# Moving the stores of converted weight tiles from SyncE's to GpSimd's DMA queue in an attention and two-layer-MLP kernel

## The chip, the cores and the metric

The kernel runs on one core of one Trainium2 chip. A core has five engines that run at the same time, each with its own instruction queue that is worked off strictly in order: TensorE (PE in the profile; its weight loads are PEld), VectorE (DVE), ScalarE (ACT), GpSimd (POOL) and SyncE (SP), which in this kernel does nothing but start transfers. Sixteen DMA engines carry the transfers. What is measured is the time of one execution on the device in microseconds (us); lower is better.

## What is computed

The reference, cut to its core: attention with rotated q and k over 2 batches of 8 heads, 576 tokens of 64 values, then two gated layers on the 1152 tokens of 512 values.

```python
scores = (q_rot @ k_rot.T) / sqrt(D); attn = softmax(scores); x = attn @ v        # 2 x 8 heads
x = x.transpose(0, 2, 1, 3).reshape(1152, 512)
x = ((x @ w_a) * (x @ w_b)) @ w_out                                               # d_ff 1536
h = x @ w_in;  out = (h * tanh(log1p(exp(h)))) @ w_out2                           # d_ff 2048
```

All weights arrive as 64-bit floats, seen by the kernel as pairs of 32-bit words. The host does no arithmetic.

## The kernel before

**Stages.** Tokens are worked batch by batch. From the start to about 100 us the attention of batch 0 runs, with its score tiles transposed by TensorE. From about 100 to 250 us the attention of batch 1 is interleaved with the first gated layer of batch 0 (`layer1(0, ...)`, then `layer2(0, ...)`): here the score tiles are split into two 16-bit halves `pp` by VectorE and transposed by transfers (`pt<-pp`, 36 of them). Then comes the first gated layer of batch 1, and from about 365 us on the last two layers (`hidden_two` and `accumulate`), which end with the output.

**Weights.** `weights` (from line 578) is called for each of 68 tiles of 128x512 values. SyncE loads the 64-bit tile `wr`; VectorE turns it into 32-bit floats `xw` by three instructions (one TENSOR_SCALAR, two SCALAR_TENSOR_TENSOR); a copy of `xw` is stored to a DRAM scratch tile, `ka` for the 24 tiles of layer one, `kb` for the 12 of its second matmul, `kc` for the 32 of the last two layers. These stores (256 KB each) are lines 601 and 607. When the second batch needs the tile, it is loaded from there (`wc<-ka` and so on) and isn't converted again. For the first use the tile is split into a rounded part and a rest: ScalarE writes the one (`w<-xw`), VectorE or GpSimd the other (`w<-xw,w`, the `any_` instruction of `weights`). Until about 250 us `wr` and `xw` have three buffers each: the fourth conversion waits until the first one's store has landed and its split is done.

**The order of the work.** Nothing is issued directly. Every call is recorded by `Plan.record`, with a cost from `Plan.cost`; `Plan.order` then runs a list scheduler over the recorded instructions, with a priority for each, and the instructions are issued to the engines in the order it gives. Instructions recorded on `any_` go to VectorE or GpSimd, by which of the two ends them earlier by the planner's account. Two instructions that read two SBUF tiles are held apart on these two engines (`op.lock`). So a change of where one instruction stands, or of what it costs in the planner, moves others on all engines.

Two names of the rows below: `qkr` are loaded q and k tiles, which are rotated into `qk` by VectorE and GpSimd (`any_` again), and `m` is the row maximum that VectorE takes of each score tile `s`.

Of the kernel before, what the change touches and what calls it, by code (L numbers as in the profile page):

```python
# [41 lines left out]
YM = 1500  # L42
D1 = 6
D4 = 2
LOOK = dict(pe=50, act=0, dve=0, pool=0, sp=0)


# [128 lines left out]
class Plan:  # L176
# [30 lines left out]
    def record(self, engine, method, args, kw):  # L207
        key = engine.key
        out = kw["out"] if "out" in kw else args[0]
        also = kw.pop("also", ())  # L210
        views = [v for v in list(args) + list(kw.values()) if isinstance(v, View)]
        deps, roots = [], []
        for v in views + list(also):
            t = v.root
            assert not t.dead, t.kw
            if t.first is not None:
                deps.append((t.first, False))
            elif t not in roots:
                roots.append(t)
                deps.append((t.pool.opened, True))  # L220
                if t.before is not None and t.before not in roots:
                    deps.append((t.before.first, False))
                if t.frees is not None:
                    t.frees.dead = True
                    deps += [(op, True) for op, *_ in t.frees.seen]
        marks = []
        for v in views:
            write, box = v is out or v is kw.get("accum_out"), v.box()
            for op, b, w, e, a in v.root.seen:
                bank = v.root.pool.space == PSUM and (key == "pe") != (e == "pe")  # L230
                if (write or w or bank) and box[0] < b[1] and b[0] < box[1] and box[2] < b[3] and b[2] < box[3]:
                    if v.root.pool.space == PSUM or v.meets(a):
                        deps.append((op, True))
            marks.append((v, box, write))
        if key == "flex":

            scale = kw["scale"]
            forms = (
                ("act", "activation", args + (AF.Copy,), dict(scale=scale)),
                ("dve", "tensor_scalar_mul", args + (scale,), {}),  # L240
            )
            method, args, kw = forms[0][1:]
        cost, dma = self.cost({"any": "dve", "flex": "act"}.get(key, key), method, out, args, kw, views)
        op = self.new(key, (engine.real, method, args, kw), deps, cost, dma, roots)
        op.wide = key == "pe" and views[1].root.dtype != F16

        ins = [v for v in views if v is not out and v is not kw.get("accum_out")]
        sb = sum(v.root.pool.space != PSUM for v in ins)
        op.lock = key in ("dve", "pool", "any") and (sb > 1 or sb == len(ins) == 1)
        if key == "any":  # L250
            op.costs = dict(dve=cost, pool=self.cost("pool", method, out, args, kw, views)[0])
        elif key == "flex":
            op.costs = {e: self.cost(e, m, out, args, {}, views)[0] for e, m, *_ in forms}
            op.call = {e: (self.real[e], m, a, k) for e, m, a, k in forms}
        for t in roots:
            t.first = op
        for v, b, w in marks:
            t = v.root
            if w and (v.a.flags.contiguous or v.n * v.a.itemsize == b[3] - b[2] or t.pool.space == PSUM):
                t.seen = [  # L260
                    s for s in t.seen if not (b[0] <= s[1][0] and s[1][1] <= b[1] and b[2] <= s[1][2] and s[1][3] <= b[3])
                ]
            t.seen.append((op, b, w, key, v.a))
        return op

    def cost(self, key, method, out, args, kw, views):

        if key == "sp":
            v = views[0]
            if method == "dma_start_transpose":  # L270
                return 1356, 1700
            return 475, int(np.prod(v.a.shape)) * v.a.itemsize / 320
        psum = any(v.root.pool.space == PSUM for v in views if v is not out)
        n = max(v.n for v in views)
        pointers = sum(v.n == 1 for v in views if v is not out) if out.n > 1 or method == "tensor_scalar" else 0
        if key == "pe":
            rhs = kw["rhs"] if method == "matmul" else args[1]
            n = rhs.n
            n *= 1 if rhs.dtype != F32 else 4 if method == "matmul" else 2
            if rhs.a.shape[0] == 64 and rhs.dtype == F32:  # L280
                n /= 2
            return n, n * rhs.a.shape[0] / 128
        if key == "act":
            return n / 1.2 + (51 if psum else 93) + 93 * min(pointers, 1), 0
        if key == "dve":
            fast = method.startswith("tensor_scalar") or method == "tensor_copy"
            if psum:
                return n / 0.96 + 65 + 58 * min(pointers, 1), 0
            return n / (1.92 if fast else 0.96) + 69 + 58 * min(pointers, 1), 0
        if key == "pool":  # L290
            return (n * 2.132 + 132 if method != "memset" else n), 0

    def order(self):
# [17 lines left out]
        while True:  # L311
# [44 lines left out]
            free[e] = start + op.cost  # L356
            if op.lock:
                held[e] = free[e]
            if e == "sp":
                tr = op.call[1] == "dma_start_transpose"  # L360
                d0 = max(dma_free, start + (1300 if tr else 1100))
                dma_free = d0 + op.dma
                if tr:
                    free[e] = max(free[e], dma_free - 1700)
                op.end = dma_free
            else:
                op.end = free[e]
            same, other = self.LAT.get(e, (0, 0))
            if e == "sp":
                same = other = 1000  # L370
            stale |= {"act", "dve", "pool"} if e in ("act", "dve", "pool") else {e}
            for nxt, data in op.after:
# [54 lines left out]
S0_AT = 20  # L427
W3S = 28
HBB = 2
EARLY = 6  # L430
S_AT = 10
GB = 6
# [48 lines left out]
def lo32(ap):  # L481
    return ap.bitcast(F32)
# [3 lines left out]
def kernel(ctx: ExitStack, tc: tile.TileContext, qk, v5, w1, w2, w34, tab, out):  # L486
# [9 lines left out]
        plan.engine(k, e)  # L496
        for k, e in dict(pe=nc.tensor, act=nc.scalar, dve=nc.vector, pool=nc.gpsimd, sp=nc.sync, any=None, flex=None).items()
    )

    def open_pool(name, bufs=1, side="left", space=None):  # L500
        kw = dict(name=name, bufs=bufs)
# [27 lines left out]
    kept = {}  # L529
# [39 lines left out]
    def weights(  # L569
# [5 lines left out]
        if cached is not None and cached in kept:  # L575
            tag = "rawc" if "rawc" in rings else "xw"
            r = rings[tag][0].tile([128, 512], F32, tag=tag, name=f"wc{i}", bufs=rings[tag][1])
            plan.release = 1000 * hold
            sp.dma_start(r, kept[cached])
            plan.release = 0  # L580
        else:
            r = rings["raw"][0].tile([128, 512], I64, tag="raw", name=f"wr{i}", bufs=rings["raw"][1])
            plan.release = 1000 * hold
            sp.dma_start(r, src)
            plan.release = 0
            words = r.bitcast(U32).rearrange("p (n t) -> p n t", t=2)
            lo, hi = words[:, :, 0], words[:, :, 1]
            x = rings["xw"][0].tile([128, 512], U32, tag="xw", name=f"xw{i}", bufs=rings["xw"][1])
            dve.tensor_scalar(x, hi, 3, 0x3FFFFFF8, op0=ALU.logical_shift_left, op1=ALU.bitwise_and)
            dve.scalar_tensor_tensor(x, hi, 0xC0000000, x, op0=ALU.bitwise_and, op1=ALU.bitwise_or)  # L590
            if plain:

                w = w_p.tile([128, 2, 512], F32R, tag="w", name=f"w{i}", bufs=6)
                dve.scalar_tensor_tensor(
                    w[:, 0, :].bitcast(U32), lo, 29, x, op0=ALU.logical_shift_right, op1=ALU.bitwise_or
                )
                if stat is not None:
                    magnitude(lo32(w[:, 0, :]), stat)
                if keep is not None:
                    kept[keep] = d_p.tile([128, 512], F32, tag=f"k{keep}", name=f"k{keep}")  # L600
                    sp.dma_start(kept[keep], lo32(w[:, 0, :]))
                return w
            dve.scalar_tensor_tensor(x, lo, 29, x, op0=ALU.logical_shift_right, op1=ALU.bitwise_or)
            r = x.bitcast(F32)
            if keep is not None:
                kept[keep] = d_p.tile([128, 512], F32, tag=f"k{keep}", name=f"k{keep}")
                sp.dma_start(kept[keep], r)
            if stat is not None:
                magnitude(r, stat)
            if top is not None:  # L610
                dve.tensor_reduce(top, r, axis=AX.X, op=ALU.max, apply_absolute_value=True)
# [958 lines left out]
```

## Time and profile before

| what | value |
|---|---|
| time, median of 3 runs | 561.01 us (559.72 to 561.78) |
| the profiled execution | 559.72 us, of which its span 557.9 us |
| PE busy | 543.5 us (97%) |
| DVE busy | 473.7 us (85%) |
| ACT busy | 356.2 us (64%) |
| POOL busy | 137.0 us (25%) |
| DMA, share of 16 engines | 69.6% on the one queue that the kernel uses |

The profile is of one execution; times count from the first instruction. An engine's busy time counts its arithmetic, not waiting and not the issue of transfers. Matmuls overlap one another, so a busy PE is not PE at its peak rate. Rows of the queue that SyncE works off are marked SPq. A line number says little here: all instructions are issued on one line (398), so the names of the tiles tell them apart; out<-in is what an instruction writes and reads.

### The profile page before, as it was taken

The page shows a single profiled execution, that of the slowest core. Times are in us where ns is not written, and L with a number is a line of the kernel's source. Part 1 is how long each engine was busy: PE and PEld are TensorE (multiplying, and loading weights), DVE is VectorE, ACT ScalarE, POOL GpSimd, SP SyncE. Part 2 cuts the span into 40 slices and gives each one's busy share as a digit, 9 for nine tenths or more (in the row PEclk, how much of TensorE's full clock was granted, in tenths as well). Part 3 has the DMA queues.
Part 4 walks back from the last instruction along what each step waited for, and adds up shares of the span by engine and source line. Part 5 has one row for each costly group of instructions (what it writes and reads, how often), then busy time and mean ns, then how long its engine had stood idle before and what let it go on. Part 6 is the DMA issues. An engine that isn't in the chain of part 4 may idle for free.

```text
span 557.9 us, 11793 instructions
## 1 busy us (share of the span) xinstructions
PE 543.5 (97%) x4416; PEld 429.0 (77%) x4416; DVE 473.7 (85%) x897; ACT 356.2 (64%) x731; POOL 137.0 (25%) x176
## 2 busy tenths in 40 slices
PE   7999999999999999999999999999999999999997
PEld 5777788889898989899777779997666776555553
DVE  5998999999999999976998999879999997554542
ACT  3879788677678786554676764459675545443440
POOL 1677657521221010110003103645420200000000
PEclk8899999999999999999999999999999999999999
DMA  8336456899999999999988379774789555421002
GB/s 317 110 102 214 166 165 177 228 229 218 290 204 241 252 260 241 236 268 376 387 274 278 102 254 344 269 242 147 264 278 326 179 189 200 137 96 60 1 0 94
DMA packets 92200, 117.40 MB, mean 210 GB/s; under 512 B 52080, under 2 KB 58224, under 8 KB 92144
## 3 DMA queue, kind: packets, MB, share of 16 engines
q1 hardware_dynamic: 92144, 116.66, 69.6%
q8 instruction: 34, 0.56, 0.4%
q14 instruction: 22, 0.18, 0.1%
HBM read 77.82 MB, written 27.53 MB: 189 GB/s over the span
## 4 chain that ended last, share of the span: by engine, by line
PE 84%; DVE 8%; ACT 3%; issue 2%; DMA 1%; POOL 1%; SPq 0%; DVEq 0%; ACTq 0%; POOLq 0%
PE l L398 38%; PE acc L398 16%; PE h L398 13%; PE s L398 8%; PE o L398 6%; PE tm L398 2%; DVE m L398 2%; DVE xw L398 1%; PE xt L398 1%; DMA qkr_k<-in_qk_dram 1%; DVE ptm L398 1%; DVE pp L398 1%; DVE wv L398 1%; DVE hb L398 1%; ACT wv L398 1%
## 5 line engine op out<-in xcount | busy, mean ns | idle before, releaser
L398 PE MATMUL l<-x,w 128*128 128x320 f32 (+3 forms) x1152 | 157.8, 294 | 0.0
L398 PE MATMUL acc<-w,g 128*128 128x512 f16 (+1 forms) x432 | 103.4, 384 | 0.0
L398 DVE SCALAR_TENSOR_TENSOR xw<-wr,xw 128x512 uint32<-128x512 uint32 x136 | 95.6, 708 | 1.0
L398 PEld LDWEIGHTS <-wv 128*128 128x128 f16 x672 | 64.7, 98 | 27.9 <-issue 5.9
L398 PE MATMUL l<-ab,w 128*128 128x320 f32 (+1 forms) x576 | 81.3, 299 | 0.1
L398 PEld LDWEIGHTS l<-x,w 128*128 128x128 f32 x576 | 78.2, 190 | 3.0 <-issue 2.7
L398 PEld LDWEIGHTS l<-ab,w 128*128 128x128 f32 x576 | 77.5, 190 | 1.2 <-issue 0.8
L398 PEld LDWEIGHTS <-w 128*128 128x128 f16 x576 | 56.1, 98 | 14.3 <-issue 0.2
L398 PEld LDWEIGHTS <-g 128*128 128x128 f16 x372 | 36.3, 98 | 36.7
L398 DVE TENSOR_TENSOR hb<-h,hb 128x256 f32<-128x256 f32 (+1 forms) x112 | 48.0, 453 | 13.5 <-PE h L398 11.9
L398 PE MATMUL h<-sp,wv 128*128 128x256 f16 (+1 forms) x384 | 57.7, 286 | 0.6 <-DVE hb L398 0.6
L398 DVE TENSOR_REDUCE m<-s 128x1 f32<-128x576 f32 x72 | 51.9, 749 | 4.4 <-PE s L398 3.9
L398 PE MATMUL s<-qk 64*128 64x288 f32 x256 | 44.8, 439 | 2.4 <-DVE qk L398 1.6
L398 ACT ACTIVATE hb<-hb,two_dn 128x512 f32<-128x512 f32 (+1 forms) x32 | 24.8, 775 | 34.1 <-DVE hb L398 34.1
L398 ACT ACTIVATE junk<-xw 128x512 f32<-128x512 f32 x51 | 32.6, 639 | 17.4 <-DVE xw L398 15.4
L398 PE MATMUL h<-y,wv 128*128 128x256 f16 (+1 forms) x288 | 43.3, 286 | 0.3 <-DVE hb L398 0.3
L398 PEld LDWEIGHTS s<-qk 64*128 64x128 f32 x256 | 25.5, 190 | 11.4 <-issue 4.9
L398 ACT ACTIVATE s<-s,m 128x576 f32<-128x576 f32 x36 | 25.3, 716 | 11.5 <-DVE m L398 11.0
L398 DVE TENSOR_SCALAR xw<-wr 128x512 uint32<-128x512 uint32 x68 | 31.7, 477 | 0.5 <-DMA wr<-in_w_dram 0.5
L398 DVE SCALAR_TENSOR_TENSOR g<-hb,g_up,g 128x640 f16<-128x640 f32 (+1 forms) x27 | 24.2, 895 | 6.3 <-ACT g L398 5.8
L398 DVE SCALAR_TENSOR_TENSOR w<-wc,o_up,w 128x512 f16<-128x512 f32 x16 | 11.9, 750 | 20.2 <-ACT w L398 20.1
L398 POOL TENSOR_TENSOR w<-xw,w 128x512 fp32r<-128x512 f32 x10 | 13.6, 1362 | 62.2 <-ACT w L398 59.1
(186 smaller groups left out, 937.5 us busy)
## 6 DMA issues: line engine op xcount, KB each, us to landing
wr<-in_w_dram SPq DMA_DIRECT2D x68, 512.0 KB, 5.3
kc<-xw SPq DMA_DIRECT2D x32, 256.0 KB, 4.2
qkr<-in_qk_dram SPq DMA_DIRECT2D x14, 576.0 KB, 4.5
wc<-kc SPq DMA_DIRECT2D x27, 256.0 KB, 3.7
ka<-xw SPq DMA_DIRECT2D x24, 256.0 KB, 3.1
wc<-ka SPq DMA_DIRECT2D x24, 256.0 KB, 5.3
wt<-kc SPq DMA_DIRECT2D x16, 256.0 KB, 3.9
kwt<-wv SPq DMA_DIRECT2D x8, 512.0 KB, 3.8
```

The source lines that it names most:

```text
L398: getattr(engine, method)(*map(real, args), **{k: real(v) for k, v in kw.items()})
```

## The change

The planner learns that a transfer may be issued from an engine other than SyncE (a table of costs, `ISSUE`), and the two stores in `weights` go to the engine that `STQ` names, which is GpSimd. All 68 stores of converted tiles move; the loads, the transposing transfers, the other stores (the 16 of `kwb` and `kwt`, and the output) stay on SyncE.

```diff
+ISSUE = dict(sp=475, act=350, pool=1000)
...
-        op.lock = key in ("dve", "pool", "any") and (sb > 1 or sb == len(ins) == 1)
+        op.lock = key in ("dve", "pool", "any") and not method.startswith("dma_start") and (sb > 1 or sb == len(ins) == 1)
...
-        if key == "sp":
+        if method.startswith("dma_start"):
...
-            return 475, int(np.prod(v.a.shape)) * v.a.itemsize / 320
+            return ISSUE[key], int(np.prod(v.a.shape)) * v.a.itemsize / 320
...
-            if e == "sp":
+            moves = op.eng != "event" and op.call[1].startswith("dma_start")
+            if moves:
...
-            if e == "sp":
+            if moves:
                 same = other = 1000
...
+STQ = "pool"
...
+    st = dict(act=act, pool=pool, sp=sp)[STQ]
...
-                    sp.dma_start(kept[keep], lo32(w[:, 0, :]))
+                    st.dma_start(kept[keep], lo32(w[:, 0, :]))
...
-                sp.dma_start(kept[keep], r)
+                st.dma_start(kept[keep], r)
```

Since the planner sees a different cost on two engines, the order changes on all of them from the first store on, and some `any_` instructions change sides. SyncE's queue a little after 100 us, before (`pt` are the transposing transfers, `wr` the loads of weights):

```order
L398 DMA_TRANSPOSE pt_1726<-pp_1686 128x9x128
L398 DMA_TRANSPOSE pt_1751<-pp_1701 128x9x128
L398 DMA ka_1775<-xw_1679 128x512
L398 DMA wr_1781<-in_w_dram 128x512
L398 DMA ka_1791<-xw_1690 128x512
L398 DMA wr_1808<-in_w_dram 128x512
L398 DMA vh_1831<-vhl_108 64x8x66 x2
```

and the same place of SyncE's queue now:

```order
L400 DMA_TRANSPOSE pt_1700<-pp_1670 128x9x128
L400 DMA_TRANSPOSE pt_1739<-pp_1696 128x9x128
L400 DMA wr_1760<-in_w_dram 128x512
L400 DMA wr_1823<-in_w_dram 128x512
L400 DMA_TRANSPOSE pt_1838<-pp_1809 128x9x128
L400 DMA_TRANSPOSE pt_1878<-pp_1817 128x9x128
L400 DMA vh_1907<-vhl_108 64x8x66 x2
```

The stores are gone from between the loads, and two transposes now stand ahead of the small copies `vh`. GpSimd's queue between about 190 and 250 us, where layer one of batch 0 ends, before:

```order
L398 TENSOR_TENSOR ab_7_0_2868<-a_sb,ab_7_0_2868 128x256
L398 TENSOR_TENSOR w_2884<-xw_2765,w_2884 128x512
L398 TENSOR_TENSOR ab_8_0_3023<-a_sb,ab_8_0_3023 128x256
L398 TENSOR_TENSOR w_3323<-xw_3250,w_3323 128x512
L398 TENSOR_TENSOR w_3403<-xw_3311,w_3403 128x512
L398 TENSOR_TENSOR w_3714<-xw_3630,w_3714 128x512
L398 TENSOR_TENSOR w_3803<-xw_3746,w_3803 128x512
```

and now, from the same tile of layer one on:

```order
L400 TENSOR_TENSOR ab_8_0_3018<-a_sb,ab_8_0_3018 128x256
L400 DMA ka_3089<-xw_3008 128x512
L400 TENSOR_TENSOR w_3116<-xw_3008,w_3116 128x512
L400 DMA ka_3157<-xw_3061 128x512
L400 DMA ka_3214<-xw_3154 128x512
L400 DMA ka_3315<-xw_3262 128x512
L400 TENSOR_TENSOR w_3334<-xw_3262,w_3334 128x512
L400 DMA kb_3359<-xw_3268 128x512
L400 DMA kb_3458<-xw_3389 128x512
L400 DMA kb_3548<-xw_3484 128x512
L400 DMA kb_3603<-xw_3490 128x512
```

Stores now fill GpSimd's queue there, and of the rests `w<-xw,w` fewer stand on it. Over the whole program the instructions that change sides between GpSimd and VectorE are these, all of them between the first store (60 us) and 250 us: of `w<-xw,w` GpSimd has 8 in place of 10; of `qk<-qkr` 128x576, 4 in place of 6; of `ab<-a_sb,ab` 128x256, 3 in place of 4; of `qkr<-qkr,cs` 128x576, 6 in place of 7; of `qkr<-qkr,cq` 128x576, 8 in place of 6. VectorE has the difference each time.

## Rows read from the trace of the kernel before

**Rows 1.** The page's first part: busy time, share of the span, instructions of each engine
```profile
span 557.9 us, 11793 instructions
PE 543.5 (97%) x4416; PEld 429.0 (77%) x4416; DVE 473.7 (85%) x897; ACT 356.2 (64%) x731; POOL 137.0 (25%) x176
```

**Rows 2.** Stretches: length, busy time of the engines named, clock, DMA share, GB/s
```profile
core 0: us, PE busy (x) PEld busy (x) DVE busy (x) ACT busy (x) POOL busy (x), PEclk, DMA share, GB/s
60.00:250.00 190.00, 186.46 (x1827) 165.91 (x1826) 180.96 (x337) 140.35 (x325) 55.34 (x61) 1.00 0.91 227
60.00:100.00 40.00, 37.84 (x427) 31.70 (x426) 37.81 (x75) 33.02 (x74) 27.63 (x37) 1.00 0.54 171
100.00:160.00 60.00, 58.75 (x534) 52.35 (x535) 58.44 (x102) 43.91 (x104) 14.05 (x13) 1.00 0.98 237
...
260.00:360.00 100.00, 100.00 (x797) 85.09 (x796) 94.51 (x186) 63.14 (x145) 18.11 (x20) 1.00 0.81 283
```

**Rows 3.** Waits of PE and DVE, 60 to 250 us: total, times, longest
```profile
PE s L398 <- DVE pp L398: 1.3, 3, 0.5
PE xt L398 <- POOL xbd L398: 0.9, 1, 0.9
...
DVE a_sb L398 <- PE l L398: 1.6, 4, 0.7
...
DVE xw L398 <- DMA wr<-in_w_dram: 0.5, 1, 0.5
...
DVE qkr L398 <- DMA qkr<-in_qk_dram: 0.4, 1, 0.4
```

**Rows 4.** Longest wait of SyncE's queue, 60 to 250 us: total, times, longest
```profile
SPq L398 <- DVE xw L398: 33.6, 19, 4.5
```

**Rows 5.** Groups of VectorE (x71, x26, x35: 60 to 250 us) and GpSimd: busy, mean ns, idle before
```profile
L398 DVE SCALAR_TENSOR_TENSOR xw<-wr,xw 128x512 uint32<-128x512 uint32 x71 | 50.3, 708 | 0.4
...
L398 DVE TENSOR_TENSOR w<-xw,w 128x512 fp32r<-128x512 f32 x26 | 20.5, 790 | 0.5 <-ACT w L398 0.4
L398 DVE TENSOR_SCALAR xw<-wr 128x512 uint32<-128x512 uint32 x35 | 16.9, 489 | 0.5 <-DMA wr<-in_w_dram 0.5
...
L398 DVE TENSOR_TENSOR qkr<-qkr,cq 128x576 f32<-128x576 f32 x8 | 6.5, 821 | 0.0
L398 DVE TENSOR_TENSOR qkr<-qkr,cs 128x576 f32<-128x576 f32 x7 | 5.3, 767 | 0.4 <-DMA qkr<-in_qk_dram 0.4
L398 DVE TENSOR_TENSOR ab<-a_sb,ab 128x256 fp32r<-128x256 f32 x8 | 4.4, 556 | 0.0
L398 DVE TENSOR_TENSOR qk<-qkr 128x576 f32<-128x576 f32 x1 | 0.8, 752 | 0.0
...
L398 POOL TENSOR_TENSOR w<-xw,w 128x512 fp32r<-128x512 f32 x10 | 13.6, 1362 | 62.2 <-ACT w L398 59.1 <-DVE a_sb L398 3.1
```

**Rows 6.** Tile xw, whole span: duration ns min/median/max, first and last start
```profile
L398 DVE SCALAR_TENSOR_TENSOR xw<-wr,xw x136: 668/684/1262, 57.0 to 457.8; 128x512 uint32<-128x512 uint32 x136
L398 DVE TENSOR_SCALAR xw<-wr x68: 367/421/1656, 56.5 to 456.6; 128x512 uint32<-128x512 uint32 x68
...
L398 DVE TENSOR_TENSOR w<-xw,w x26: 667/687/1796, 80.3 to 248.5; 128x512 fp32r<-128x512 f32 x26
L398 SPq DMA_DIRECT2D ka<-xw x24: 326/339/1343, 60.5 to 200.5; - x24
```

**Rows 7.** Timelines of DVE, SPq and POOL, 104 to 123 us: start, duration, instruction
```profile
111.71 1.66 DVE L398 TENSOR_SCALAR xw<-wr 128x512 uint32<-128x512 uint32 x1
...
122.06 0.41 DVE L398 TENSOR_SCALAR xw<-wr 128x512 uint32<-128x512 uint32 x1
...
116.03 0.57 SPq L398 DMA_DIRECT2D ka<-xw  x1
...
111.12 1.97 POOL L398 TENSOR_TENSOR qkr<-qkr,cs 128x576 f32<-128x576 f32 x1
```

**Rows 8.** The page's DMA issues: count, KB each, median us from issue to landing
```profile
ka<-xw SPq DMA_DIRECT2D x24, 256.0 KB, 3.1
```

## The prediction

> **What bounds the kernel now.** I read the page's first part, then the busy times by stretch, then who waits for whom. PE is busy 97% of the span [rows 1], so at most some 14 us of the 557.9 are PE idle, and part of that is the start. The stores of the change begin at 60 us [rows 6], so I looked from there on. From 60 to 250 us PE is busy 186.5 of 190 us and DVE 181.0 [rows 2]: two engines are nearly full together, with 3.5 and 9.0 us of holes. From 260 to 360 us PE is at 100 of 100 us and DVE at 94.5, so there PE alone sets the pace and passes a delay on unchanged. The waits between 60 and 250 us say the same [rows 3]: PE's longest in total is 1.3 us, for DVE, and none of its waits is for a transfer. DVE waits for transfers twice, 0.5 us for a load of weights and 0.4 us for one of q and k. What DVE has to do between 60 and 250 us is therefore what another instruction there is charged to.
>
> SyncE's queue looks bad at first sight: it stands 33.6 us waiting for a conversion `xw` to end before it can issue a store, with loads and transposes behind it [rows 4]. But a wait counts only if somebody waits for what stands behind it, and rows 3 say that nobody does, but for 0.9 us.
>
> **The change part by part.**
>
> *SyncE's queue loses 68 stores.* 36 of them (24 `ka`, 12 `kb`) lie before 250 us, at 0.34 us of issue each [rows 6], 12.2 us together, plus the 33.6 us of waiting. The loads behind them start earlier, as far as their buffers allow. The gain is bounded by what DVE waits for transfers, 0.9 us, since PE waits for none. I take 0, with −0.9 as the end.
>
> *VectorE gets arithmetic that stood on GpSimd.* By the counts of the order and the means of rows 5: two `w<-xw,w` at 0.790, two `qk` at 0.752, one `ab` at 0.556, one `qkr,cs` at 0.767, and two `qkr,cq` fewer at 0.821. That is 1.58 + 1.50 + 0.56 + 0.77 − 1.64 = +2.8 us of DVE, all between 60 and 250 us. GpSimd loses four instructions net, 4 × 1.36 = 5.4 us by the mean of its `w`.
>
> The two engines also disturb each other. At 111.71 us DVE's TENSOR_SCALAR took 1.66 us in place of its median of 0.42 and ended just after POOL's instruction of 111.12 us, which took 1.97 [rows 6, 7]. Priced by mean against median [rows 5, 6], DVE loses 26 × 0.103 = 2.7 us on `w`, 35 × 0.068 = 2.4 us on TENSOR_SCALAR and 71 × 0.024 = 1.7 us on the other conversions, 6.8 us while POOL is busy for 55.3 us [rows 2]: 0.12 us for each us of POOL. The four instructions that leave POOL so give DVE 5.4 × 0.12 = 0.6 us back.
>
> *GpSimd gets 36 stores before 250 us and 32 after.* No row shows a transfer issued by POOL, so I bound it. From below: a store has no operand that POOL's arithmetic reads, and may cost DVE nothing, 0. From above: it occupies POOL like an arithmetic instruction on a tile of that size, 1.36 us [rows 5], and disturbs DVE at the same rate: 36 × 1.36 × 0.12 = 5.9 us. The nearest row is the same transfer issued by SyncE, 0.34 us [rows 6]: 36 × 0.34 × 0.12 = 1.5 us, which I take. The 32 `kc` stores fall where PE is full and DVE has some 5% to spare [rows 2]; I cost them at 0. If that cover is gone, they are 32 × 0.34 × 0.12 = 1.3 us.
>
> *Buffers.* The `xw` ring holds three tiles, so a store that lands late stops a conversion, and everything behind it on DVE. The store issued at 116.03 us empties the buffer that DVE writes again at 122.06 us [rows 7]. A store lands 3.1 us after its issue [rows 8], so 2.9 us are left, in what is among the tightest of the 36 cases. POOL may delay a store that long without anyone noticing. I cost it at 0.
>
> Here a rule speaks against the change. The trace shows how work of POOL and an instruction of DVE shut each other out for over a microsecond [rows 7]. The Trainium skill, page "SBUF — State Buffer", section "SBUF: two separate sides", says that the descriptors of a DMA issued from GpSimd are written by GpSimd's own cores, which are locked out while VectorE runs an instruction in a two-port mode; under "A bandwidth-pool intuition that's wrong" it tells of such a DMA that took 620 ns alone and 3100 beside one. By it, as an estimate, a store would land 2.5 us later, still inside the 2.9 us left, and the sum would stay as it is. No run shows it yet; it bears on the first rival.
>
> *The sum.* DVE gets +2.8 − 0.6 + 1.5 = +3.7 us between 60 and 250 us. How much reaches the end? At least nothing, if its 9.0 us of holes take it all; at most all. DVE is busy 95% there, nearer to full than to free, and some of the holes are waits for PE (1.6 us in the longest row of rows 3), which shrink as DVE falls behind. I take two thirds, +2.5 us. On the profiled run of 559.72 us (span 557.9 and 1.8 around it) this gives 562.2. That run lies 1.3 us under the median of the three, and a median is what is asked, so the forecast is 561.0 + 2.5 = **563.5 us**. Its own range is 561.3 to 566: at the low end a third of 2.2 (no store term) and half of the 0.9 us of loads saved, at the high end the whole 3.7 with the 1.3 of the `kc` stores.
>
> **The rivals.**
>
> *GpSimd and VectorE get in each other's way, slower.* Every store occupies POOL like a full instruction. Then the store term is 5.9 in place of 1.5, and DVE's plus is 8.1 us, about as much as all its holes, so that most work waits for it and it passes nearly whole: 561.0 + 8.1 = 569.1 us. Such a store decides from about 0.7 us on POOL, where its term of 3.0 brings DVE's plus to 5. It grows if POOL's queue gets late by more than the 2.9 us of the ring, since DVE then stands in front of a conversion: six stores late by half a microsecond beyond that are 3 us more. For it: the 1.66 us of rows 7, and a queue in which stores that wait for DVE now stand ahead of `xbd` and `xn`, which lead to PE's transposes. Against it: POOL is busy only 55 of 190 us [rows 2], and what PE waits for it is 0.9 us, once [rows 3].
>
> *The loosened queue pays, faster.* Loads run ahead, two tiles are converted in a row, and the order that the planner finds for DVE, ACT and PE with less in SyncE's way is the tighter one. What there is to gain is PE's idle time from 60 to 250 us, 3.5 us, of which 2.2 lie before 100 us and 1.3 before 160 [rows 2]. All of it gives 557.5 us. For it: 33.6 us of waiting vanish from SyncE's queue [rows 4]. Against it: DVE has more to do than before, and nobody waits for a load [rows 3]. The Trainium skill, page "Perfetto Trace Analysis", section "DMA Optimizations", holds that it may make sense to give loads to one issuing engine and stores to another; no row here shows it to be worth more than this.
>
> *Nothing moves.* DVE's holes take up what is added, 561.0 us.
>
> **How the numbers follow.** The forecast, 45%; stores that cost POOL and DVE dearly, 25%; faster, 20%; nothing moves, 10%. A measurement of this kernel can tell about 0.5% from no change, so the limits are 558.2 and 563.8. Faster: the second rival, 0.20. Same: the 10% of the last and 28 of the forecast's 45, together 0.38. Slower: the other 17 and the 25 of the first rival, 0.42. To hold the time eight times in ten the range must reach into both rivals: from 556.5 (all of PE's idle time, the 0.9 us of loads and a little) to 572 (the first rival with its ring term).
>
> **What would show it.** Right: DVE's busy time up by 3 to 4 us before 260 us, medians of `w` and TENSOR_SCALAR unchanged, no wait of DVE for a `ka` store, a span longer by 2 to 4 us, all of it there when the first batch's layer one ends. The first rival: means of the conversions well over 0.49 and 0.71 us, or waits of DVE or ACT for POOL or for `ka<-xw`. The second: PE's 3.5 us of idle time gone. I would be wrong altogether with a loss that arises after 260 us, where I cost everything at nothing, or with stores that land far later than 6 us after their issue.

## The result, and the profile after

The changed kernel takes **563.74 us** in the median (563.41 to 566.73), the kernel before 561.1 beside it: ratio 1.0057 with a 95% interval of 1.0032 to 1.0082. A second comparison gave 1.0041 [1.0021, 1.0061]. The change costs 2.3 to 3.2 us. The forecast was 563.5. The number is right; of the steps that led to it, several are not.

The first part of the page after (busy time, share of the span, instructions), to be held against [rows 1]:

```profile
span 561.8 us, 11874 instructions
...
PE 545.5 (97%) x4416; PEld 429.9 (77%) x4416; DVE 473.7 (84%) x901; ACT 355.7 (63%) x731; POOL 170.1 (30%) x240
```

DVE has its four additional instructions (901 for 897), and yet its busy time is the same to a tenth. It should have risen by 3.7 us. POOL has 33.1 us more: the profile counts the issue of a store as busy time on GpSimd, which it does not on SyncE. The 68 stores are 38.2 us of it (18.0 and 13.7 in the rows below, and 6.5 for the 12 `kb`); POOL's arithmetic fell by 5.1.

The stretches after, as in [rows 2], and the one in which the second loss lies (in the kernel before it reads PE 19.42, DVE 19.06):

```profile
core 0: us, PE busy (x) PEld busy (x) DVE busy (x) ACT busy (x) POOL busy (x), PEclk, DMA share, GB/s
60.00:250.00 190.00, 185.45 (x1787) 163.29 (x1786) 179.10 (x340) 139.38 (x324) 69.44 (x92) 1.00 0.90 223
...
260.00:360.00 100.00, 100.00 (x797) 85.12 (x796) 91.07 (x184) 62.26 (x142) 25.47 (x39) 1.00 0.82 285
380.00:400.00 20.00, 18.05 (x135) 13.00 (x134) 18.25 (x40) 16.61 (x27) 10.06 (x11) 1.00 0.62 196
```

From 380 to 400 us PE stands idle 1.95 us in place of 0.58. From 60 to 250 us DVE is busy less, not more; but a window of fixed length holds less work when the kernel is late, so a total over the span is the safer figure.

Waits after, 60 to 250 us (total, times, longest), to be held against [rows 3, 4]:

```profile
POOL ka L400 <- DVE xw L400: 48.5, 16, 5.7
POOL kb L400 <- DVE xw L400: 35.7, 9, 6.0
...
PEld L400 <- DMA pt<-pp: 1.4, 2, 1.1
...
DVE xw L400 <- DMA kb<-xw: 1.1, 1, 1.1
PE o L400 <- DMA pt<-pp: 0.8, 1, 0.8
```

The waiting for conversions has gone from SyncE's queue to GpSimd's. New are a wait of DVE for a store (the ring of `xw`) and waits of PE for transposes, which the first profile of before had none of. The groups and landing times of the stores after (xcount, busy us, mean ns; KB, median us to landing), and VectorE's conversions from 60 to 250 us, to be held against [rows 5, 6, 8]:

```profile
L400 POOL DMA_DIRECT2D kc<-xw x32 | 18.0, 562 | 117.5 <-DVE xw L400 99.2
...
L400 POOL DMA_DIRECT2D ka<-xw x24 | 13.7, 573 | 60.8 <-DVE xw L400 48.5
...
kc<-xw POOLq DMA_DIRECT2D x32, 256.0 KB, 5.4
...
ka<-xw POOLq DMA_DIRECT2D x24, 256.0 KB, 4.5
```

```profile
L400 DVE SCALAR_TENSOR_TENSOR xw<-wr,xw 128x512 uint32<-128x512 uint32 x70 | 49.0, 702 | 0.4
...
L400 DVE TENSOR_TENSOR w<-xw,w 128x512 fp32r<-128x512 f32 x27 | 19.6, 726 | 0.3 <-ACT w L400 0.3
...
L400 DVE TENSOR_SCALAR xw<-wr 128x512 uint32<-128x512 uint32 x35 | 15.1, 439 | 1.1 <-DMA kb<-xw 1.1
```

A `ka` store takes POOL 0.57 us on average and lands 1.4 us later than before (4.5 for 3.1). The means of all three conversions fell.

### The profile page after: what moved, and what is told of

The parts are those of the page before. It is cut to its first block, busy times and chain, and to the rows that moved or that the text cites. A ratio compares the mean times of both kernels' runs of the same rounds, so it can differ in the third digit from the quotient of the medians.

```text
span 561.8 us, 11874 instructions
## 1 busy us (share of the span) xinstructions
PE 545.5 (97%) x4416; PEld 429.9 (77%) x4416; DVE 473.7 (84%) x901; ACT 355.7 (63%) x731; POOL 170.1 (30%) x240
## 3 DMA queue, kind: packets, MB, share of 16 engines
q0 software_dynamic: 5440, 17.83, 8.4%
## 4 chain that ended last, share of the span: by engine, by line
PE 81%; DVE 7%; ACT 4%; DMA 3%; issue 3%; POOL 0%; SPq 0%; DVEq 0%; ACTq 0%; POOLq 0%
PE l L400 33%; PE acc L400 17%; PE h L400 14%; PE s L400 8%; PE o L400 6%; PE tm L400 2%; DMA pt<-pp 2%; DVE m L400 2%; DVE xw L400 1%; DVE w L400 1%; DMA qkr_k<-in_qk_dram 1%; PE xt L400 1%; DVE pp L400 1%; ACT ptm L400 1%; ACT e L400 0%
## 5 line engine op out<-in xcount | busy, mean ns | idle before, releaser
L400 POOL DMA_DIRECT2D kc<-xw x32 | 18.0, 562 | 117.5 <-DVE xw L400 99.2
L400 POOL DMA_DIRECT2D ka<-xw x24 | 13.7, 573 | 60.8 <-DVE xw L400 48.5
L400 DVE TENSOR_SCALAR xw<-wr 128x512 uint32<-128x512 uint32 x68 | 28.6, 429 | 2.7 <-DMA kc<-xw 1.5
```

Source lines behind the costliest of these rows:

```text
L400: getattr(engine, method)(*map(real, args), **{k: real(v) for k, v in kw.items()})
```

## Where the loss lies: the program cut at fixed matmuls

Windows of fixed time mix work and delay, so each trace was also cut at four matmuls that every version has: the 65th `s<-qk` (at 47 us), the first `l<-x,w` of the second batch (265 us), the first `h<-y,wv` (370 us) and the 101st (420 us); the end is the last `acc`. (In e2 and e4 the start alone took over 2 us longer, so that the first cut lies at 49.9 and 49.4 us; the pieces leave that out.) The runs e1 to e12 are told below. Length of each piece in us, by the starts of these matmuls:

```
order of      stores on                   run      47-265  265-370  370-420  420-end
before        SyncE                       before   216.47   104.76    50.06   135.23
before        SyncE                       e5       217.59   104.95    50.20   135.22
before        ScalarE                     e9       216.61   104.74    50.28   135.34
before        ka kb on GpSimd             e7       218.99   104.73    50.04   135.23
before        kc but two on GpSimd        e11      217.84   104.73    50.10   135.17
before        kc on GpSimd                e8       219.61   104.73    51.04   135.19
before        GpSimd                      e1       218.65   104.73    51.04   135.21
after         SyncE                       e2       218.41   104.73    51.36   135.04
after         GpSimd                      after    219.26   104.73    51.22   135.04
after         GpSimd                      e6       219.53   104.73    51.17   135.03
after, 1 move GpSimd                      e12      219.91   104.73    51.59   135.04
own, ka kb    ka kb on GpSimd             e3       220.00   104.73    51.99   135.33
own, kc       kc on GpSimd                e4       219.21   104.73    55.90   134.96
own, kc       SyncE                       e10      217.55   104.75    51.38   135.06
```

Where PE is full, from 265 to 370 us and from 420 us on, the pieces agree to 0.4 us. The loss has two places. **From 370 to 420 us** it is 1.1 us (51.2 for 50.1). The kernels with the order of before take 50.04 to 50.28 us there, or 51.04, twice; those with the order of after 51.17 to 51.36. **From 47 to 265 us** it is about 1.6 us on average. The orders of e4 and e10 part from that of before, and that of e3 from that of after, only behind 260 us, so their rows count here too: 219.26, 219.53, 219.91 and 220.00 (e3) against 216.47, 217.55 (e10), 217.59, 217.84, 219.21 (e4) and 219.61, whose stores before 250 us are all on SyncE. But the same instructions take 216.5 in one execution and 219.6 in another. 1.1 + 1.6 = 2.7, between the two measured losses.

## The experiments

In e1, e2 and e7 to e11 `Engine(plan, key, nc.x)` records a call with the cost and queue that the planner has for `key` and issues it on `nc.x`: so the order can be kept while the queue changes, and the other way round. Where a line of `dma_start` is edited, only one of the two stores is shown; the other is edited alike. Ratios are to the kernel before, measured beside each run; behind them stands the 95% interval.

**Queue and order apart.** e1 keeps the order of before on PE, DVE and ACT word for word and issues the stores on GpSimd; e2 has the order of after, with the stores on SyncE.

```diff
-    st = dict(act=act, pool=pool, sp=sp)[STQ]
+    st = Engine(plan, "sp", nc.gpsimd)      # e1
+    st = Engine(plan, "pool", nc.sync)      # e2
```

> The planner charges the stores to SyncE as before, but they are issued from GpSimd: PE, DVE and ACT have the order of before word for word, GpSimd has its arithmetic of before with the 68 stores between it. Theory O (the new order costs, not the queue): 561.1 within 1 us, transposes land a median 4.2 us after their issue as before. Theory Q (stores on a second queue delay the transposing transfers): 563 to 565, transposes land at 4.8 us as in the changed kernel, PE waits for pt. My sum of the prediction (instructions moved to VectorE cost 2.8 us, stores 1.5): nothing moved here, so 561 to 562.

> The planner charges the stores to GpSimd as in the changed kernel, so that PE, DVE and ACT have its order word for word, but they are issued from SyncE. Theory O: 563.7 within 1 us, with the two waits of the changed kernel in place (pt near 200 and 230 us, the stretched VectorE instruction near 366 us). Theory Q: 561 within 1 us, transposes landing at 4.2 us. My sum: as theory O, 563 to 564, since the moved instructions are all there.

e1: ratio 1.0014 [0.9997, 1.0031]; e2: 1.0025 [1.0005, 1.0045]. Neither alone comes to the 1.0041 to 1.0057 of both, but each interval reaches down to almost nothing, and that of e2 up to 1.0045. In e1 PE waited 2.4 us for `pt`, in e2 not at all, which seemed to say that the queue delays the transposes.

**Only some of the stores moved, with the order the planner then makes.** e3 moves `ka` and `kb`, e4 `kc`.

```diff
-                    st.dma_start(kept[keep], lo32(w[:, 0, :]))
+                    (pool if keep[0] in "ab" else sp).dma_start(kept[keep], lo32(w[:, 0, :]))   # e3
+                    (pool if keep[0] == "c" else sp).dma_start(kept[keep], lo32(w[:, 0, :]))    # e4
```

> Only the 36 stores before 250 us are issued (and planned) on GpSimd, the 32 kc stores stay on SyncE. Both theories expect the loss that the changed kernel has by 253 us, 3.1 us, and not the 1.0 us that it gains at 366 to 390 us: 564 less 1, about 563 to 564. If the order is a matter of chance, the loss by 253 us can differ by some us, since 541 lines of PE differ from before and 55 from the changed kernel.

> Only the 32 kc stores are issued (and planned) on GpSimd; up to 250 us the order is nearly that of before. Both theories: no loss by 253 us and the 1.0 us of 366 to 390 us, 562.1. My sum had this part at 0, 561.1.

e3: 1.0065 [1.0043, 1.0088]; e4: 1.0107 [1.0077, 1.0137]. e3 loses 3.7 us where 2 to 3 were expected, e4 6 where 1 was. Half of the change costs more than the whole, so the parts don't add up: each has an order of its own in its later part. In e4 most of it lies between 370 and 420 us (55.90), and the stretches of e4 show how a small loss becomes a large one:

```profile
core 0: us, PE busy (x) PEld busy (x) DVE busy (x) ACT busy (x) POOL busy (x), PEclk, DMA share, GB/s
380.00:390.00 10.00, 6.40 (x52) 5.02 (x52) 9.51 (x17) 7.71 (x11) 6.44 (x7) 0.96 0.72 251
390.00:400.00 10.00, 9.71 (x53) 6.31 (x52) 7.90 (x16) 7.61 (x14) 2.84 (x4) 0.70 0.32 93
```

PE was busy only 6.40 of 10 us while DVE was full, and after that the granted clock stood at 0.70, a mix of its two levels, 2.4 and 1.2 GHz. Ten microseconds at 0.70 lose 3.0.

**Both kernels once more.** e5 is the kernel before, e6 the changed one.

> The kernel before, unchanged, profiled once more. It tells whether the first profile was a lucky one at the two places where the profile after falls back. Theory Q (a second queue for the stores delays the transposes pt<-pp): PE idle time from 190 to 250 us again below 0.5 us (0.13 in the first profile), no wait of PE for pt, landing of pt 4.2 us. Theory N (the first profile was lucky, the place itself is unsteady): 1 us or more of PE idle time there and waits of PE for pt of 0.8 us or more, with the stores all on SyncE. Time ratio 1.000 by both.

> The changed kernel, unchanged, on the same chip as the parts. Queue and order together: ratio 1.003 to 1.008 (1.0057 in the first comparison). The profile should again show about 1.5 us of PE idle time from 190 to 250 us with waits for pt<-pp, and about 2 us of it from 380 to 390 us (1.95 in the first profile); if either is gone by a microsecond, that loss is not a fixed one. DVE busy from 60 to 250 us 179 us, again below the 180.96 of before; by the sum of the prediction it would be 184.6.

e5: 0.9996 [0.9978, 1.0013]; e6: 1.0041 [1.0021, 1.0061]. The second profile of before has 1.12 us of PE idle time from 190 to 250 us (58.88 busy of 60) where the first had 0.13, and 1.0 us of waiting for `pt`. So theory N holds: the first profile was lucky there, and a part of what the profile after seemed to lose in that place belongs to both. The loss at 370 to 420 us came again (51.17 for 51.22).

**The queue alone, in two parts.** The order of before; e7 moves only `ka` and `kb`, e8 only `kc`.

```diff
+    st = Engine(plan, "sp", nc.gpsimd)
...
+                    (st if keep[0] in "ab" else sp).dma_start(kept[keep], lo32(w[:, 0, :]))   # e7
+                    (st if keep[0] in "c" else sp).dma_start(kept[keep], lo32(w[:, 0, :]))    # e8
```

> The order of the kernel before on PE, DVE and ACT, word for word; only the 36 stores ka and kb are issued on GpSimd, the 32 stores kc stay on SyncE. Theory Q: the loss before 253 us is all here: PE waits for pt<-pp from 190 to 250 us by 1 to 3 us, landing of pt 4.6 us or more (4.2 before), nothing new after 360 us, ratio 1.001 to 1.004. Theory O (it is the new order that costs): no wait of PE for pt above 0.5 us, ratio 0.9985 to 1.0015.

> The order of the kernel before on PE, DVE and ACT, word for word; only the 32 stores kc are issued on GpSimd. Theory Q: nothing before 253 us; from 360 to 400 us the stores, which wait on GpSimd's queue for DVE's conversions, hold the wx arithmetic behind them: PE idle there 1 us more than the 0.94 of before, ratio 1.001 to 1.003. Theory O: the same 0.94 us or less within 0.5, ratio 0.9985 to 1.0015. The forecast's own term for these stores was 0, with 1.3 us (ratio 1.0023) if PE's cover were gone.

e7: 0.9996 [0.9979, 1.0012], although its profile has the waits that theory Q expects. PE's waits for `pt`, 60 to 250 us, first in e7, then in e8, whose stores before 250 us are all on SyncE:

```profile
PE o L400 <- DMA pt<-pp: 2.7, 4, 1.2
```

```profile
PE o L400 <- DMA pt<-pp: 1.9, 2, 1.0
```

Such waits come with the stores on either queue. Over 14 profiles they are longer when `ka` and `kb` are on GpSimd (0.8 to 3.0 us, 2.1 on average in six) than when not (0 to 1.9, 0.7 in eight), but the time of e7 allows the queue at most 0.12% there, 0.7 us. Theory Q falls as far as it was to explain more.

e8: 1.0020 [0.9999, 1.0041], and 51.04 us from 370 to 420 us, to the hundredth what e1 has. Here theory Q's second half holds in the time: with the `kc` stores on GpSimd the piece took 1 us more in these two executions, where I had costed them at 0; e11 below shows that it need not. VectorE and GpSimd around the 25th `kc` store, in e8 (start, duration, instruction, idle before):

```profile
362.61 0.72 DVE L400 SCALAR_TENSOR_TENSOR xw<-wr,xw 128x512 uint32<-128x512 uint32 x1
363.25 0.41 DVE L400 TENSOR_REDUCE y_mx<-l 128x1 f32<-128x256 f32 x1
363.59 3.04 DVE L400 TENSOR_SCALAR xw<-wr 128x512 uint32<-128x512 uint32 x2
366.55 1.62 DVE L400 SCALAR_TENSOR_TENSOR wv<-wt,two_up,wv 128x512 f16<-128x512 f32 x2
```

```profile
363.63 0.56 POOL L400 DMA_DIRECT2D kc<-xw  x1 [0.84 <-DVE xw L400]
364.21 0.75 POOL L400 TENSOR_TENSOR wx<-wt,wt 128x256 f32<-128x256 f32 x1
364.91 0.73 POOL L400 TENSOR_TENSOR wx<-wt 128x256 f32<-128x256 f32 x1
365.61 1.61 POOL L400 TENSOR_TENSOR wx<-wt,wx 128x256 f32<-128x256 f32 x2
```

and the same instructions in the kernel before:

```profile
359.39 0.42 DVE L398 TENSOR_REDUCE y_mx<-l 128x1 f32<-128x256 f32 x1
359.73 1.60 DVE L398 TENSOR_SCALAR xw<-wr 128x512 uint32<-128x512 uint32 x2
361.50 1.86 DVE L398 SCALAR_TENSOR_TENSOR wv<-wt,two_up,wv 128x512 f16<-128x512 f32 x2 [0.17 <-ACT wv L398]
```

```profile
359.42 0.74 POOL L398 TENSOR_TENSOR wx<-wt,wt 128x256 f32<-128x256 f32 x1
360.12 0.92 POOL L398 TENSOR_TENSOR wx<-wt 128x256 f32<-128x256 f32 x1
361.01 2.07 POOL L398 TENSOR_TENSOR wx<-wt,wx 128x256 f32<-128x256 f32 x2
```

In e8 the store waits on GpSimd's queue for the conversion (the one of 362.61) to end, and four `wx` instructions stand behind it. They run off in one train after it, and DVE's next conversion, which would have run at the same moment, stands still while three of them run: the pair of TENSOR_SCALARs takes 3.04 us for 1.60, and the second of them alone 2.71. In the kernel before the four run off in one train too (359.42 to 363.08 us), but directly behind a copy of `y`, no store between, and no TENSOR_SCALAR takes over 0.96 us beside them. e1, e8 and e11 all have this 2.7 us instruction, the four others in the order of before don't. It isn't the store that shuts DVE out, but the arithmetic that the waiting store has set beside DVE's next conversion.

**A second queue that is not GpSimd's.** Order of before, all 68 stores on ScalarE.

```diff
+    st = Engine(plan, "sp", nc.scalar)
```

> The order of the kernel before, word for word; all 68 stores are issued on ScalarE's queue in place of GpSimd's. Theory G (the loss after 360 us comes from GpSimd's arithmetic standing behind waiting stores): GpSimd is free, so from the first h matmul to the 101st it takes 50.1 to 50.2 us as before, not the 51.04 of the two kernels with kc on GpSimd. Theory Q (any second queue does it): 51.0 us there. Theory A: ScalarE's own arithmetic stands behind the waiting stores, as GpSimd's did, and that costs more than on GpSimd, since ScalarE is busy 64% and GpSimd 25%: ratio above 1.003, with PE waiting for ACT.

Ratio 0.9993 [0.9969, 1.0018], 50.28 us from 370 to 420: theory G holds, Q and A fall. The stores land as late as from GpSimd (issues of e9: KB, median us to landing), and the time shows nothing of it:

```profile
kc<-xw ACTq DMA_DIRECT2D x32, 256.0 KB, 5.6
...
ka<-xw ACTq DMA_DIRECT2D x24, 256.0 KB, 4.4
```

PE's waits for ScalarE from 60 to 250 us are 0.6 us in e9 and in the kernel before, and ScalarE's busy time is 355.0 us (356.2 before). That `junk` and `w`, which stand behind the stores there, need the same conversions is the likely reason, but no run was made for it.

**The order of e4 without its queue.**

```diff
+    st = Engine(plan, "pool", nc.sync)
...
+                    (st if keep[0] == "c" else sp).dma_start(kept[keep], lo32(w[:, 0, :]))
```

> The order that the planner makes when only the stores kc are on GpSimd (the kernel that was 1.0107 of before), but with all stores issued on SyncE. If the order alone costs it: ratio again 1.008 or more, and the stretch from the first to the 101st h matmul again about 55.9 us with a granted clock below 1.00 between 390 and 400 us. If it is GpSimd's queue: that stretch 50 to 51.5 us, ratio below 1.004.

Ratio 1.0013 [0.9995, 1.0032], 51.38 us: the order alone costs 1.3 us there, the queue alone 1.0 (e8, in the order of before), both together 5.8. PE's idle time in the piece is 2.41 us in e10 and 3.89 in e4; these 1.5 and the 3.0 of the clock are the 4.5 between the two. PE's longest waits from 376 to 392 us in e4:

```profile
PE h L400 <- DVE hb L400: 1.7, 1, 1.7
PE o_scale L400 <- DVE hb L400: 1.2, 1, 1.2
```

**All `kc` stores but two.** As e8, with the 26th and 27th, which stand in front of the last `wx` train, on SyncE.

```diff
+                    (st if keep[0] == "c" and sum(k[0] == "c" for k in kept) not in (26, 27) else sp).dma_start(kept[keep], r)
```

> The order of the kernel before, word for word; of the 32 stores kc 30 are issued on GpSimd, the 26th and 27th (at 367 us before) stay on SyncE. If these two hold GpSimd's wx and y,y instructions back, which then stretch DVE's wv: PE's gap of 1.15 us in front of h<-y,wv (63rd matmul of the stretch) goes to 0.3 us or less, the stretch to the 101st h matmul from 51.04 back to 50.1 to 50.2 us, ratio 1.000. If it is the sum of all kc stores on GpSimd: the 1.15 us and 51.0 us stay.

Ratio 0.9998 [0.9979, 1.0018], 50.10 us, the gap of 1.15 us is 0.19. That is the number that the theory wanted, but not by its route. The two stores hold nothing back in e8: the `wx` behind them waits for a load, `wt<-kc`, half a microsecond after they are through.

```profile
371.87 1.14 POOL L400 DMA_DIRECT2D kc<-xw  x2 [4.65 <-DVE xw L400]
373.55 0.73 POOL L400 TENSOR_TENSOR wx<-wt,wt 128x256 f32<-128x256 f32 x1 [0.53 <-DMA wt<-kc]
```

What decides is a second collision, on the `wv` of 128x256 in front of the gap, with GpSimd's second `s<-y,y`. First e8, then e11:

```profile
378.86 1.18 DVE L400 SCALAR_TENSOR_TENSOR wv<-wt,two_up,wv 128x256 f16<-128x256 f32 x1
378.87 0.88 POOL L400 TENSOR_TENSOR s<-y,y 128x320 f32<-128x320 f32 x1 [0.49 <-ACT y L400]
```

```profile
376.61 0.47 DVE L400 SCALAR_TENSOR_TENSOR wv<-wt,two_up,wv 128x256 f16<-128x256 f32 x1
376.89 0.94 POOL L400 TENSOR_TENSOR s<-y,y 128x320 f32<-128x320 f32 x1 [0.75 <-ACT y L400]
```

In e11 the `wv` starts 0.27 us ahead of GpSimd's instruction and takes 0.47 us, in e8 it starts 0.02 ahead and takes 1.18. So a quarter of a microsecond is worth nothing or 1 us. The traces show where it comes from. Relative to the first `h<-y,wv`, DVE is late after the 2.7 us conversion, by 0.9 us in e11, 1.15 in e8 and 1.3 in e1. A load `wt<-kc` is issued 0.7 to 0.8 us after an earlier `wv` of DVE ends, in the kernel before as in these, and so comes late too: it lands 1.5, 1.8 and 1.9 us behind that `h`, and 0.8 ahead of it in the kernel before. The next train of `wx` waits for the load, and the later it runs, the longer takes a `wv` of 128x1024 beside it (1.29 us in e11, 1.54 in e8), which stands ahead of the one that decides. The quarter is there before the two stores are issued, and up to then e8 and e11 run the same instructions on the same queues: it is a difference between executions, and taking the two stores away didn't bring it. So the `kc` stores on GpSimd bring the 2.7 us conversion in three executions of three, and the loss of 1 us in two of them. In e5, with all stores on SyncE, the same `wv` starts 0.17 us ahead of the same GpSimd instruction, and nothing is lost.

**One instruction of the new order moved back.** The changed kernel; `wv0_6_0` on ScalarE, which its order puts between the two halves of `hb`, goes back behind them.

```diff
         self.done = self.order()
...
+        i, j = names.index("wv0_6_0"), names.index("w100")
+        op = self.done.pop(i)
+        self.done.insert(j, op)
```

> The changed kernel with one instruction of ScalarE moved back by four: wv<-wt,two_up 128x512, which its order puts between the two halves of hb at 383.7 us, stands behind them as in the kernel before; all else word for word. If this instruction is what the new order loses there: the two gaps of PE at the 98th and 99th matmul (0.58 for ACT w, 0.49 for ACT hb) shrink by 0.7 us together or more, the stretch from the first to the 101st h matmul goes from 51.2 to 50.5 us or less, ratio about 0.001 to 0.002 below the changed kernel's 1.004 to 1.006. If not: the same two gaps and 51.2 us.

Ratio 1.0048 [1.0031, 1.0066], 51.59 us: the theory falls. PE's waits from 380 to 395 us, after and in e12:

```profile
PE h L400 <- DVE hb L400: 0.6, 1, 0.6
PE acc L400 <- ACT w L400: 0.6, 1, 0.6
PE h L400 <- ACT hb L400: 0.5, 1, 0.5
PE h L400 <- DVE o L400: 0.2, 1, 0.2
```

```profile
PE h L404 <- DVE hb L404: 1.2, 3, 0.7
PE h L404 <- ACT hb L404: 0.5, 1, 0.5
PE h L404 <- DVE o L404: 0.2, 1, 0.2
PE acc L404 <- ACT w L404: 0.2, 1, 0.2
```

The wait for `w` shrank by 0.4 us as meant, and waits for DVE's `hb` took its place.

## Why the number was right, and which steps were not

*SyncE's queue freed: 0.* Right, net. In the same order (e2 against after and e6) with the stores on GpSimd PE is 1.5 us ahead by 115 us, counted from 47 us; by 172 us the whole of it is given back; why, no run shows. The rival "the loosened queue pays" is seen to begin and to end. In e9 the 68 stores have another issuing engine than the loads, and it changes nothing that can be measured (0.9993). The Trainium skill, "Perfetto Trace Analysis", section "DMA Optimizations", holds that it may make sense to separate the two so; here it is worth nothing.

*Arithmetic moved to VectorE: +2.8, −0.6 for fewer locks.* The instructions moved as counted; the second term was mis-sized. From 60 to 250 us the means fell from 489, 790 and 708 ns [rows 5] to 439, 726 and 702: 35 × 0.050 + 27 × 0.064 + 70 × 0.006 = 3.9 us given back. The rate that I took, 0.12 us of DVE per us of POOL, put what the conversions lose over all of POOL's work, and gave 0.6. What brought the 3.9 is not shown: in e1, where no instruction leaves POOL, TENSOR_SCALAR fell to 431 ns as well and POOL's arithmetic by 3.8 us, so when the two engines meet counts, and not only how much POOL has to do. Over the whole span the two terms cancel: 473.7 us before and after, 475.1 and 474.1 in the second profiles.

*36 stores on GpSimd: 1.5 of a range from 0 to 5.9.* The low end was right. 49 conversions of DVE ran beside a store and beside no arithmetic of POOL after the change, and they are no longer for it: TENSOR_SCALAR 0.418 us on average beside a store (21 of them) and 0.416 beside nothing (37), SCALAR_TENSOR_TENSOR 0.684 (24) and 0.682 (89), `w` 0.681 (4) and 0.680 (18). Beside POOL's arithmetic they take 0.498, 0.862 and 0.890. The first rival priced the store as POOL's arithmetic and falls. The Trainium skill, "SBUF — State Buffer", sections "SBUF: two separate sides" and "A bandwidth-pool intuition that's wrong", tells of a transfer issued by GpSimd that starves beside a VectorE instruction in a two-port mode, 3100 ns for 620. Nothing of that kind is seen here, though no run shows which mode VectorE's instructions ran in: no store took POOL more than 0.77 us, and the later landing is the same from ScalarE's queue (4.4 and 5.6 us for 4.5 and 5.4), which by that page no such lock reaches.

*The buffers: 0.* Nearly right: one wait of DVE for `kb`, 1.1 us (0.5 in e6), that the 2.9 us of slack did not cover; none for `ka`. 1.5 us of waiting for `kc` lie where PE is the bound.

*32 `kc` stores: 0, or 1.3 if PE's cover is gone.* This is the step that failed, and I had written that a loss after 260 us would make me wrong altogether. PE covers everything from 265 to 370 us, as taken. It does not from 370 to 420 us, where before it idles 0.9 us in front of `h` and waits for DVE; I read the windows to 360 us and took the rest to be like them. What the stores do there is also another thing than in the price: what counts is not their issue time but the wait of each for a conversion, in an in-order queue with arithmetic behind it, and that costs 1 us or nothing (e1 and e8, e11). In the changed kernel itself the new order loses as much in that piece without the queue (e2: 51.36) as with it (51.22, 51.17), by other gaps: 0.6, 0.6 and 0.5 us in front of `h`, `acc` and `h`, which e2 has to within 0.02 us. I know that it is the order, and not which of its instructions.

*Two thirds of +3.7 us of DVE, all by 250 us.* That this came to 2.5 is an accident: the sum of DVE is 0, and what was lost is 1.1 us after 370 us and about 1.6 before 265. For the latter neither order nor queue alone shows enough (218.4; 218.65 and 218.99, against 218.0 on average), and executions of the same instructions differ by 3.1 us. The 14 profiles hint at a share of each. PE's idle time from 190 to 250 us is 1.5 to 2.8 us (2.4 on average) in the six with `ka` and `kb` on GpSimd and 0.1 to 2.1 (1.0) in the others. The piece less this idle time is 216.1 to 217.5 us with the order that before has up to there and 217.2 to 217.9 with the new one. It stays open what of the 1.6 us is which.

## What to carry to other kernels

Issuing a transfer on an engine with arithmetic in its queue puts its wait for the producer into that queue: look not at the time that the issue takes but at what stands behind it, and at what that will run beside once it is released. Read the windows of the whole program, the short ones between two full stretches too, and cost a part at nothing only where PE is full in its own piece. Where a planner reorders everything, compare queue and order in separate kernels, cut the traces at fixed instructions, and profile the kernel before twice: its own spread at a place is the smallest loss that a pair of profiles can show there.

## What was not expected of the hardware

A store issued by GpSimd takes its engine 0.56 us in the median, against 0.34 on SyncE [rows 6], and the 49 conversions of VectorE that ran beside one were no longer for it. The same 68 stores, 17.83 MB, are 5440 packets from GpSimd's queue and 9792 from ScalarE's. In the same order and on the same queue, PE's idle time from 190 to 250 us, in e5 and e8 nearly all of it waits for the transposes, goes from 0.13 over 1.12 to 2.12 us from one execution to the next (before, e5, e8), which is most of the 3.1 us that tell the first and the last of these apart in the piece from 47 to 265 us.
